# Zero-weight column-tiled matmuls in TensorE's idle gaps, and score matmuls over 32 rows

## The chip, the cores and the metric

The kernel runs on one core of one Trainium2 chip. The metric is the device time of one execution in microseconds (us). The comparison is between the kernel as it stands (called before) and the kernel with one change (called after), on the same inputs.

## The reference, cut to what matters

Attention with 32 query heads that share one key and one value head, and a GELU MLP, both fed by the same layer norm and added to the input:

```python
def _A_ref(x, wq, wk, wv, wo):              # x: 1 x 2048 x 512, H = 32 heads of Dh = 16
    q = (x @ wq).reshape(B, S, H, Dh).transpose(0, 2, 1, 3)
    k = x @ wk                              # one key head, one value head
    v = x @ wv
    scores = jnp.einsum("bhqd,bkd->bhqk", q, k) * (Dh ** -0.5)
    p = _softmax(scores, axis=-1)
    o = jnp.einsum("bhqk,bkd->bhqd", p, v)
    return o.transpose(0, 2, 1, 3).reshape(B, S, H * Dh) @ wo

def _B_ref(x, w1, b1, w2, b2):              # w1: 512 x 1792, w2: 1792 x 512
    h = _gelu(jnp.einsum("bsd,df->bsf", x, w1) + b1)
    return jnp.einsum("bsf,fd->bsd", h, w2) + b2

xn = _layernorm(x, axis=-1)
return x + _A_ref(xn, ...) + _B_ref(xn, ...)
```

Everything is bfloat16 outside. The exponentials of the scores are 32 x 2048 x 2048 elements, and they are the bulk of the elementwise work.

## The kernel before: how the work is tiled and ordered

**Stages.** A prologue (to about 45 us) normalises x, transposes it into `xnT`, and makes the keys `KT`, the values `V1` and the first queries `QT`. Then the main loop runs to about 857 us, and a short tail projects and stores the last tiles.

**The main loop.** Queries go in 4 blocks of 512 and heads in 8 groups of 4, so there are 32 groups (`gg`). One group has 64 score tiles: 16 key tiles of 128 by 4 heads. A tile is 128 keys x 512 queries and fills one PSUM bank. Three tiles make one unit `u`, and there are 683 units. `scores(u)` (line 660) is three matmuls of 17 rows, one for each of three heads, which lie in different 32-row strips of the array: rows `q0` to `q0 + 17` of `KT` and `QT`, where the 17th row carries a bound on the maximum and the rest of the 32 rows of `KT` and `QT` hold zeros. Even units write banks 0 to 2, odd units banks 3 to 5. `exp(u)` (line 680) is one ScalarE instruction over the two or three tiles of the unit that go to ScalarE (1024 or 1536 columns, written to `E`). At most one tile of a unit is marked `is_d` and goes to VectorE instead: `p1` (line 703) turns its scores into an integer whose bits are a rough exponential, and `close_batch` (line 717) adds four shifted copies, so that five matmuls make up a better one. Either way the tile is then multiplied by the values in `pv_mm` (line 712): a matmul that uses one of four 32-column strips of the array (a column-tiled matmul) and adds to bank 6, `pO`. Four such matmuls, one to each strip, run side by side.

**Side work.** The other column-tiled matmuls go through `mm4` (line 448) to bank 7, `pM`: the queries of later groups (`q_group`, `q_m`), the first MLP product (`h_mm`), the second with the output projection (`out_tile`, `y_tile`, `part_tile`). Each `pM` result is read out by a VectorE instruction with `allow=EV_ALLOW` (-2.0), a priority ahead of most other VectorE work but behind `p1` (`P1_ALLOW`, -20). At the end of a group `o_evac` (line 734) copies `pO` out on VectorE, and a chain of small DMAs on SyncE's queue brings the reciprocal of the denominators back for the normalisation. The GELU runs as a Tanh on ScalarE over up to 1536 columns (line 804), between the exponentials.

**What sets the order.** All engines run in order. The order is made when the program is built, by a planner of its own: `Prog.add` (line 59) records each operation with an assumed duration `occ`, latency `lat` and an `allow`; `Prog.schedule` (line 148) plays these forward in time, engine by engine, and `pick_pe` (line 117) chooses TensorE's next operation: scores first, column-tiled work in between, and no column-tiled work when a score is due within `S_WAIT`. A column-tiled matmul counts 0.216 us of its strip, a change between row-tiled scores and column-tiled work counts `SWITCH`. The planner of before takes TensorE as always at full clock. `Prog.emit` then writes the waits. There is a hook for filler matmuls (lines 190 to 201 and 959 to 961), which `FILL_GAP = 0` leaves off:

```python
        if FILL_GAP:
            pr.filler = lambda e: e.matmul(pO, zeros[:], xnT[:, 0, 0:TBW], start=False, stop=False, skip_group_check=True)
```

Of the kernel before, what the change touches and what calls it, by code (L numbers as in the profile page):

```python
# [10 lines left out]
P = 128  # L11
# [6 lines left out]
SPL_D = -107.78043958019079  # L18
SPL_MIN = 64.0
SWITCH = 0.1  # L20

ETA = 0.97
D_LEAD = 0.0
D_PEN = 0.3
D_TAIL = 10
D_FIRST = 3
FILL_GAP = 0
PV_MIN = 2
PV_S = 1
P1_ALLOW = -20.0  # L30
EV_ALLOW = -2.0
S_WAIT = 0.1
P_WAIT = 0.0
NE_ND_KB = (20,8,3)


class _Op:
    __slots__ = ("eng", "fn", "deps", "sdeps", "stream", "amt", "need", "ticket", "waits", "clock", "occ", "lat",
                 "allow", "kind", "tag", "nun", "outs", "rel", "rdy", "start", "end", "vis", "idx", "done")


class Prog:
# [5 lines left out]
    def __init__(self, nc):  # L48
        self.nc = nc
        self.ops = []  # L50
        self.writer = {}
        self.readers = {}
        self.accs = {}
        self.chain = {}
        self.in_chain = True
        self.filler = None
        self.fill_gap = None

    def add(self, eng, fn, r=(), w=(), acc=None, dma=None, occ=0.1, lat=0.15, allow=1.0, kind=None, tag=None, after=()):
# [88 lines left out]
    def schedule(self):  # L148
# [10 lines left out]
        ready = {e: [] for e in engs}  # L159
# [5 lines left out]
        mode = None  # L165
        cgbusy = [0.0] * 4
        visit = 0
        pend = 0.0
        accn = {}
        for op in ops:  # L170
# [7 lines left out]
        while left:  # L178
# [8 lines left out]
            e, t = best_e, best_t  # L187
            cand = [o for o in ready[e] if o.rdy <= t + 1e-9]
            if e == "pe":
                if self.filler is not None and opened is not None and t - free["pe"] > self.fill_gap and free["pe"] > 5:  # L190
                    f = _Op()
                    f.eng, f.stream, f.amt, f.need, f.ticket, f.deps, f.kind = "pe", "pe", 1, False, None, [], "fill"
                    f.fn = self.filler
                    f.start = max([free["pe"]] + cgbusy)
                    f.occ = 0.21
                    f.end = f.vis = f.start + f.occ
                    free["pe"] = f.end
                    mode = "full"
                    order.append(f)
                    nfill += 1  # L200
                    continue
                op = self.pick_pe(t, cand, ready["pe"], mode, visit, cgbusy)
# [12 lines left out]
            if e == "pe":  # L215
                st = t
                if op.kind in ("pv", "side"):
                    cg = op.tag[1]
                    st = max(t, cgbusy[cg], free["pe"])
                    if mode != "col":  # L220
                        st = max([t, pend + SWITCH] + [c + SWITCH for c in cgbusy])
                    op.start = st
                    cgbusy[cg] = st + 0.216
                    op.end = st + 0.006
                    op.vis = st + op.occ + op.lat
                    mode = "col"
                    g = op.tag[0]
                if op.kind == "pv":
                    n = accn[g] = accn[g] - 1
                    s = started.setdefault(g, {})  # L230
                    s[cg] = s.get(cg, 0) + 1
                    op.tag = (g, cg, s[cg] == 1)
                    if len(s) == 4:
                        opened = g
                    if n == 0:
                        opened = None
                elif op.kind != "side":
# [4 lines left out]
                    op.end = st + op.occ  # L242
                    op.vis = op.end + op.lat
                    if m == "col":
# [27 lines left out]
        self.nfill = nfill  # L272
        self.span = max(o.vis for o in order)
        self.ops = order

# [44 lines left out]
def bass_parallel_sum__grouped_kv_mqa__dense_activation_gelu__prompt_kernel(  # L320
# [34 lines left out]
    with ExitStack() as es:  # L355
# [276 lines left out]
                 r=["V1", "Vf"], w=[("V", 1 + v)])  # L632
        warm(4, 3)

        pool(lambda e: e.memset(zeros[:], 0.0), w=["zeros"])
# [24 lines left out]
        def scores(u):  # L660
            ts = list(range(3 * u, min(3 * u + 3, NTILE)))
            x = u % 2
            pieces, r = [], ["KTall"]
            for i, t in enumerate(ts):
                gg, kt, j = tile_of(t)
                tb, g = divmod(gg, NGR)
                q0 = 32 * j
                pieces.append((bank(3 * x + i), KT[q0:q0 + 17, kt * P:(kt + 1) * P], QT[q0:q0 + 17, g, :], q0))
                r += [("KT", kt // 4), ("QT", g), ("QTm", g, j)]

            def fn(e):
                for o, l, rh, q0 in pieces:
                    ins = e.matmul(o, l, rh, start=True, stop=True, tile_position=(q0, 0))  # L673
                return ins
            return add("pe", fn, r, [B(3 * x + i) for i in range(3)], occ=0.216, lat=0.22, allow=-1.0, kind="S")
# [281 lines left out]
            store(tb, i)  # L957
        pr.in_chain = False
        if FILL_GAP:
            pr.filler = lambda e: e.matmul(pO, zeros[:], xnT[:, 0, 0:TBW], start=False, stop=False, skip_group_check=True)  # L960
            pr.fill_gap = FILL_GAP
        fin = add("sp", None, r=[("ob", i) for i in range(4)], after=list(pr.ops))
        pr.schedule()
        global LAST
# [30 lines left out]
```

## Time and profile before

| what | value |
|---|---|
| time, median of 3 runs (873.56, 880.84, 873.33) | 873.56 us |
| the profiled execution's own time | 878.26 us |
| its span, first to last instruction | 876.4 us (1.9 us lie around it) |
| mean granted TensorE clock | 0.934 |
| busy: PE, VectorE (DVE), ScalarE (ACT) | 801.6, 751.7, 788.6 us |
| chain that ended last, by engine | ACT 51%, PE 33%, DVE 14% |

How to read it: PE's busy time is modelled with each matmul's pipeline latency, so a full share does not mean full use. The granted clock (PEclk) is the share of full speed that TensorE's clock gate let through in a stretch; it reads 1.00 or 0.50, or a mean over both. In the chain of work that ended last, the exponentials (L692) have 49% of the span. "Idle before" is the time that an engine stood still ahead of an instruction, with the engine whose result ended it.

### The profile page before, as it was taken

Reading aid. Unit: us, or ns where it says so; the run is one execution under the profiler, and the core shown is the slowest. Engines: PE = TensorE matmul, PEld = TensorE weight load, DVE = VectorE, ACT = ScalarE, POOL = GpSimd, SP = SyncE. Lnnn points to the kernel's source line nnn. Section 1 sums busy time; section 2 is a strip of 40 time slices with the busy share of each in tenths; the row PEclk is TensorE's granted clock in tenths of the full one; section 3 lists DMA queues with packets and bytes.
Section 4 is the critical chain, followed back from the end, with each engine's and each line's share of the span. In section 5 each row is a group of like instructions: output and inputs, shape, how many; then the busy total and the mean of one; then the engine's idle time right before and its main releaser. Section 6 shows DMA issues by size and latency. Waiting matters only on the chain.

```text
span 876.4 us, 20514 instructions
## 1 busy us (share of the span) xinstructions
PE 801.6 (91%) x8766; PEld 238.4 (27%) x8768; DVE 751.7 (86%) x1429; ACT 788.6 (90%) x731; POOL 25.5 (3%) x51
## 2 busy tenths in 40 slices
PE   3788999999899999998989999989989999999997
PEld 1312222222222322322222322322222332222223
DVE  7259897887988869999998968999889968999985
ACT  3378999889999899999999999999899999999981
POOL 7030000000000000000000000000000000000000
PEclk9668998779889999999999999998889999999999
DMA  8000000000000010000000100000000000000000
GB/s 289 1 25 3 15 13 14 13 15 14 2 14 20 21 26 9 21 2 14 15 13 15 27 20 9 15 14 14 15 14 15 26 20 8 15 15 14 15 14 25
DMA packets 23971, 19.02 MB, mean 22 GB/s; under 512 B 12369, under 2 KB 19402, under 8 KB 23882
## 3 DMA queue, kind: packets, MB, share of 16 engines
q1 hardware_dynamic: 22826, 17.69, 7.0%
q8 instruction: 69, 1.13, 0.5%
q10 hardware_dynamic: 1056, 0.03, 0.1%
q14 instruction: 20, 0.16, 0.1%
HBM read 14.98 MB, written 2.35 MB: 20 GB/s over the span
## 4 chain that ended last, share of the span: by engine, by line
ACT 51%; PE 33%; DVE 14%; issue 1%; DMA 0%; DVEq 0%; ACTq 0%
ACT E L692 49%; PE pAll L713 12%; PE pAll L451 10%; PE pAll L673 9%; DVE Dt L709 4%; DVE Dt L723 4%; PE pAll L445 2%; ACT ub L804 1%; DVE hb L790 1%; ACT xnT L544 1%; DVE stats L503 1%; DVE Of L736 0%; DVE ub L806 0%; DVE ub L801 0%; DVE ub L803 0%
## 5 line engine op out<-in xcount | busy, mean ns | idle before, releaser
L692 ACT ACTIVATE E<-pAll 128x1024 bf16<-128x1024 f32 (+1 forms) x683 | 751.2, 1295 | 44.7 <-PE pAll L673 39.9
L713 PE MATMUL pAll<-Dt,V 128*32 128x512 bf16 x2075 | 340.4, 401 | 2.5 <-DVE Dt L709 1.2
L709 DVE TENSOR_SCALAR Dt<-pAll 128x512 int16<-128x512 f32 x415 | 278.6, 682 | 60.7 <-PE pAll L673 56.6
L673 PE MATMUL pAll<-QT,KT 17*128 17x512 bf16 x2048 | 277.5, 400 | 43.5 <-ACT E L692 36.7
L713 PE MATMUL pAll<-E,V 128*32 128x512 bf16 x1633 | 309.1, 404 | 2.0 <-DVE Of L736 1.4
L723 DVE TENSOR_SCALAR Dt<-Dt 128x1536 int16<-128x1536 int16 (+2 forms) x588 | 282.8, 525 | 1.0
L673 PEld LDWEIGHTS pAll<-QT,KT 17*128 17x128 bf16 x2048 | 67.5, 91 | 329.2 <-ACT E L692 276.0
L713 PEld LDWEIGHTS pAll<-Dt,V 128*32 128x32 bf16 x2075 | 93.5, 98 | 98.4 <-issue 46.8
L451 PE MATMUL pAll<-w_sb,ub 128*32 128x512 bf16 x896 | 111.0, 391 | 0.0
L713 PEld LDWEIGHTS pAll<-E,V 128*32 128x32 bf16 x1633 | 74.3, 96 | 76.6 <-issue 56.4
L451 PE MATMUL pAll<-xnT,w_sb 128*32 128x512 bf16 x896 | 81.2, 400 | 1.3 <-DVE hb L790 1.0
L451 PE MATMUL pAll<-wop,oT 128*32 128x512 bf16 x512 | 70.1, 381 | 1.9 <-DVE x_sb L839 1.9
L451 PE MATMUL pAll<-xnT,wqp 128*32 128x512 bf16 x496 | 50.1, 442 | 0.5 <-DVE hb L790 0.3
L790 DVE TENSOR_SCALAR hb<-pAll,b1T 128x512 bf16<-128x512 f32 x56 | 41.3, 737 | 7.3 <-PE pAll L451 7.2
L451 PEld LDWEIGHTS pAll<-w_sb,ub 128*32 128x32 bf16 x896 | 28.8, 96 | 25.6 <-issue 15.9
L575 DVE CAST QT<-pAll 128x512 bf16<-128x512 f32 x32 | 21.8, 683 | 13.9 <-PE pAll L451 10.1
L804 ACT ACTIVATE ub<-ub 128x1536 bf16<-128x1536 bf16 (+1 forms) x20 | 30.6, 1531 | 0.0
L451 PEld LDWEIGHTS pAll<-xnT,w_sb 128*32 128x32 bf16 x896 | 21.2, 97 | 30.8 <-issue 15.1
L451 PEld LDWEIGHTS pAll<-wop,oT 128*32 128x32 bf16 x512 | 20.0, 95 | 15.7 <-issue 5.9
L541 PE MATMUL pAll<-ident,ub 128*128 128x128 bf16 x64 | 8.2, 282 | 14.9 <-POOL ub L527 10.7
L736 DVE COPY Of<-pAll 128x512 f32<-128x512 f32 x31 | 21.1, 680 | 0.1
L747 DVE TENSOR_TENSOR oT<-Of,rbc 128x512 bf16<-128x512 f32 x31 | 21.0, 679 | 0.0
(91 smaller groups left out, 254.1 us busy)
## 6 DMA issues: line engine op xcount, KB each, us to landing
rbc<-rden_rows SPq DMA_DIRECT2D x124, 64.0 KB, 2.0
w_sb<-in_B_w_dram SPq DMA_DIRECT2D x2, 1792.0 KB, 12.1
x_sb<-in_A_x_dram SPq DMA_DIRECT2D x8, 256.0 KB, 4.7
out_dram<-x_sb SPq DMA_DIRECT2D x16, 128.0 KB, 1.7
QT<-mT SPq DMA_DIRECT2D x60, 2.0 KB
ub<-in_A_wq_dram SPq DMA_DIRECT2D x1, 512.0 KB, 6.5
wop<-in_A_wo_dram SPq DMA_DIRECT2D x4, 128.0 KB, 2.7
den<-Of SPq DMA_DIRECT2D x31, 8.0 KB
```

The costliest lines, as they stand in the source:

```text
L445: return add("pe", lambda e: e.matmul(o, l, rh, start=start, stop=stop, **kw), r, w, occ=occ, lat=0.23, allow=allow, kind=kind, tag=tag)
L451: add("pe", lambda e, c=c, j=j: e.matmul(o[c, :], l[:, c], rh, start=start, stop=stop, tile_position=(0, 32 * j)), r, [(k, j) for k in w] ...
L575: dve(lambda e: e.tensor_copy(QT[:, hq, :], bank(bk)), w=[B(bk)] + [(B(bk), j) for j in range(4)] + [ ("QT", hq)] + [("QTm", hq, j) for j ...
L673: ins = e.matmul(o, l, rh, start=True, stop=True, tile_position=(q0, 0))
L692: exps.append(act(lambda e: e.activation(E[:, s0:s0 + na, :], bank(b0, na).rearrange("p (a n) -> p a n", a=na), ACT.Exp, scale=LN2 / 128.0 ...
L709: dve(lambda e: e.tensor_scalar(Dt[:, KZ, s, :], bank(bk), float(127 * 128) + SPL_D, SPL_MIN, ALU.add, ALU.max), w=[B(bk), ("D", s, KZ)], ...
L713: add("pe", lambda e, a, b: e.matmul(pO[32 * j:32 * j + 32, :], V1[:, v, kt, :], rhs, start=a, stop=b, tile_position=(0, 32 * j)), r=r + [ ...
L723: dve(lambda e, k=k: e.tensor_scalar(Dt[:, k, s0:s0 + n, :], Dt[:, KZ, s0:s0 + n, :], float(SPL_K[k]), None, ALU.add), r=[("D", s0 + i, KZ ...
L736: dve(lambda e: e.tensor_copy(Of[:, i, :], pO), w=["O", ("Of", i)], allow=0.0)
L747: onorm[gg] = dve(lambda e: e.tensor_tensor(oT[:, gg % NOT, :], Of[:, i, :], rbc[:, i, :], ALU.mult), r=[("Of", i)] + [("rbc", i, j) for j ...
L790: dve(lambda e: e.tensor_scalar(hb[:, ft % 6, :], pM, b1T[:, ft:ft + 1], None, ALU.add), r=["b1T"], w=M4 + [("h", ft % 6)], allow=EV_ALLOW)
L804: act(lambda e: e.activation(uu, uu, ACT.Tanh, scale=GELU_K), r=uk, w=uk, n=c, allow=2.5, kind="tanh")
```

## The change

The fillers are switched on and made over, the score matmuls take all 32 rows of their strip, and the planner follows a model of the clock gate. The words that come with the change also say that `pM` is read out first on VectorE.

- **Fillers.** A filler is now a set of four matmuls, one to each 32-column strip, with 128 x 32 zeros as weights and 512 columns of `xnT` as data. Where a group has `pO` open in all four strips it adds zero to `pO`; otherwise, where the last operation on `pM` was a VectorE read that has finished, it writes zeros to `pM`. The planner puts a set wherever, in its own time, TensorE would otherwise wait more than `FILL_GAP` = 0.25 us for the next score, less than `FILL_U` = 0.8 of the last `WIN` = 3.413 us was used (a column-tiled matmul counts a quarter of its 0.2133 us, a unit's scores 0.75 of theirs), and the time is past `FILL_FROM` = 60.
- **The clock in the planner.** The planner counts the same use in fixed windows of 3.413 us and doubles TensorE's durations in the window behind one with less than `HAM_T` = 0.35. So the order of the other work moves a little as well.
- **Scores.** `KT[q0:q0+32]` and `QT[q0:q0+32]` in place of 17 rows. The added rows are zero in both.

The program has 576 fillers, 144 sets. No other instruction is added or removed on any engine.

```diff
+WIN = 3.413
+HAM_T = 0.35
+HAM_PHASE = 1.5
-FILL_GAP = 0
+FILL_GAP = 0.25
+FILL_U = 0.8
+FILL_FROM = 60.0
...
+        op.pm = any(k == ("bank", 7) or k[0] == ("bank", 7) for k in w)
...
             if e == "pe":
-                if self.filler is not None and opened is not None and t - free["pe"] > self.fill_gap and free["pe"] > 5:
-                    f = _Op()
...
+                op = self.pick_pe(t, cand, ready["pe"], mode, visit, cgbusy)
+                st = max([free["pe"]] + cgbusy) if mode == "col" else max([free["pe"], pend + SWITCH] + cgbusy)
+                while recent and recent[0][0] < st - WIN:
+                    recent.pop(0)
+                low = sum(a for _, a in recent) < FILL_U * WIN
+                lim = min([o.rdy for o in ready["pe"] if o.kind == "S"] + [t + 9.0]) if op is None else t
+                tgt = pO_open = opened is not None
+                if not tgt and pmev is not None and pmev.vis <= st:
+                    tgt = True
+                if FILL_GAP and op is not None and isinstance(op, float):
+                    tgt = False
+                if FILL_GAP and tgt and low and st > FILL_FROM and lim - st > FILL_GAP:
+                    for cg in range(4):
+                        f = _Op()
...
+                        f.deps = list(self.fill_deps) if pO_open else self.fill_deps + [pmev]
+                        f.fn = (lambda e, cg=cg, o=pO_open: self.filler(e, cg, o))
+                        f.occ = 0.216 * slow
...
             if e == "pe":
-                pend = op.start + op.occ
+                while op.start > wend:
+                    slow = 1.0 if area > HAM_T * WIN else 2.0
+                    ncold += slow > 1
+                    area, wend = 0.0, wend + WIN
+                pend = op.start + op.occ * slow
...
+            if op.pm:
+                pmev = op if e == "dve" else None
+                if pmev is not None:
+                    op.need = True
...
-                pieces.append((bank(3 * x + i), KT[q0:q0 + 17, kt * P:(kt + 1) * P], QT[q0:q0 + 17, g, :], q0))
+                pieces.append((bank(3 * x + i), KT[q0:q0 + 32, kt * P:(kt + 1) * P], QT[q0:q0 + 32, g, :], q0))
...
         if FILL_GAP:
-            pr.filler = lambda e: e.matmul(pO, zeros[:], xnT[:, 0, 0:TBW], start=False, stop=False, skip_group_check=True)
+            pr.filler = lambda e, j, o: e.matmul((pO if o else pM)[32 * j:32 * j + 32, :], zeros[:, 0:32], xnT[:, 0, 0:TBW],
+                                                 start=not o, stop=not o, skip_group_check=True,
+                                                 tile_position=(0, 32 * j))
```

Two places on TensorE show what this does to the order. In the rows, `QT,KT` are scores (three matmuls are one unit), `E,V` and `Dt,V` are `pv_mm`, `xnT,w_sb` is the first MLP product, `w_sb,ub` the second, and `xnT,zeros` are the fillers.

The first place is the 87th unit, around 151 us of the profile, where a Tanh on ScalarE holds the next scores up. TensorE before:

```order
L673 MATMUL pAll<-QT,KT 128x512 x3
L713 MATMUL pAll<-Dt,V 32x512 x3
L713 MATMUL pAll<-E,V 32x512
L713 MATMUL pAll<-Dt,V 32x512 x5
L713 MATMUL pAll<-E,V 32x512
L673 MATMUL pAll<-QT,KT 128x512 x3
L713 MATMUL pAll<-E,V 32x512 x4
L673 MATMUL pAll<-QT,KT 128x512 x3
```

TensorE after, from the second of those scores:

```order
L717 MATMUL pAll<-QT,KT 128x512 x3
L757 MATMUL pAll<-E,V 32x512 x4
L1004 MATMUL pAll<-xnT,zeros 32x512 x32
L717 MATMUL pAll<-QT,KT 128x512 x3
L757 MATMUL pAll<-E,V 32x512 x3
L1004 MATMUL pAll<-xnT,zeros 32x512 x4
L717 MATMUL pAll<-QT,KT 128x512 x3
L1004 MATMUL pAll<-xnT,zeros 32x512 x4
```

Eight filler sets stand between the four value matmuls and the next scores, and one set more behind each of the two units that follow.

The second place is the 344th unit, around 456 us, at the end of a group. TensorE before, where four units of scores stand next to each other:

```order
L673 MATMUL pAll<-QT,KT 128x512 x3
L713 MATMUL pAll<-E,V 32x512 x3
L673 MATMUL pAll<-QT,KT 128x512 x12
L713 MATMUL pAll<-E,V 32x512
L673 MATMUL pAll<-QT,KT 128x512 x3
L451 MATMUL pAll<-w_sb,ub 32x512 x12
```

TensorE after:

```order
L717 MATMUL pAll<-QT,KT 128x512 x3
L757 MATMUL pAll<-E,V 32x512 x3
L1004 MATMUL pAll<-xnT,zeros 32x512 x4
L717 MATMUL pAll<-QT,KT 128x512 x3
L1004 MATMUL pAll<-xnT,zeros 32x512 x4
L757 MATMUL pAll<-E,V 32x512
L717 MATMUL pAll<-QT,KT 128x512 x3
L1004 MATMUL pAll<-xnT,zeros 32x512 x8
L757 MATMUL pAll<-E,V 32x512 x3
L757 MATMUL pAll<-Dt,V 32x512
```

Here sets have come in, and value matmuls stand between scores that followed each other directly before.

More of the change, by code (lines that the diff above doesn't have):

```diff
@@ L33 @@
 P_WAIT = 0.0
-NE_ND_KB = (20,8,3)
+NE_ND_KB = (20, 8, 3)
 class _Op:
     __slots__ = ("eng", "fn", "deps", "sdeps", "stream", "amt", "need", "ticket", "waits", "clock", "occ", "lat",
-                 "allow", "kind", "tag", "nun", "outs", "rel", "rdy", "start", "end", "vis", "idx", "done")
+                 "allow", "kind", "tag", "nun", "outs", "rel", "pm", "rdy", "start", "end", "vis", "idx", "done")
 class Prog:
@@ L57, in __init__ @@
         self.fill_gap = None
+        self.fill_deps = []
+        self.log = []
     def add(self, eng, fn, r=(), w=(), acc=None, dma=None, occ=0.1, lat=0.15, allow=1.0, kind=None, tag=None, after=()):
@@ L167, in schedule @@
         visit = 0
+        recent = []
+        pmev = None
+        area, wend, slow = 0.0, HAM_PHASE, 2.0
+        ncold = 0
         pend = 0.0
@@ L189, in schedule @@
             if e == "pe":
-                if self.filler is not None and opened is not None and t - free["pe"] > self.fill_gap and free["pe"] > 5:
-                    f = _Op()
[L192 to L199, printed above, removed]
+                op = self.pick_pe(t, cand, ready["pe"], mode, visit, cgbusy)
@@ new lines, in schedule @@
+                if FILL_GAP and op is not None and isinstance(op, float):
[3 more added lines that the diff above has]
+                        f = _Op()
+                        f.eng, f.stream, f.amt, f.need, f.ticket, f.kind = "pe", "pe", 1, False, None, "fill"
+                        f.deps = list(self.fill_deps) if pO_open else self.fill_deps + [pmev]
+                        f.fn = (lambda e, cg=cg, o=pO_open: self.filler(e, cg, o))
+                        f.tag = (None, cg)
+                        f.occ = 0.216 * slow
+                        f.start, f.end, f.vis = st, st + 0.006, st + f.occ
+                        order.append(f)
+                        recent.append((st, 0.0533))
+                        cgbusy[cg] = st + f.occ
+                    area += 0.2133
+                    pend = st + f.occ
+                    mode = "col"
+                    free["pe"] = max(free["pe"], st + 0.02)
@@ L200, in schedule @@
                     nfill += 1
                     continue
-                op = self.pick_pe(t, cand, ready["pe"], mode, visit, cgbusy)
+                if op == "idle":
+                    op = None
                 if op is None or isinstance(op, float):
@@ L222, in schedule @@
                     op.start = st
-                    cgbusy[cg] = st + 0.216
+                    cgbusy[cg] = st + 0.216 * slow
+                    area += 0.0533
+                    recent.append((st, 0.0533))
                     op.end = st + 0.006
-                    op.vis = st + op.occ + op.lat
+                    op.vis = st + op.occ * slow + op.lat
                     mode = "col"
@@ L241, in schedule @@
                     op.start = st
-                    op.end = st + op.occ
+                    op.end = st + op.occ * slow
                     op.vis = op.end + op.lat
+                    area += op.occ * (0.75 if op.kind == "S" else 1.0)
+                    recent.append((st, op.occ * (0.75 if op.kind == "S" else 1.0)))
                     if m == "col":
@@ L272, in schedule @@
         self.nfill = nfill
+        self.ncold = ncold
         self.span = max(o.vis for o in order)
@@ L633, in bass_parallel_sum__grouped_kv_mqa__dense_activation_gelu__prompt_kernel @@
         warm(4, 3)
-        pool(lambda e: e.memset(zeros[:], 0.0), w=["zeros"])
+        zop = pool(lambda e: e.memset(zeros[:], 0.0), w=["zeros"])
         pool(lambda e: e.memset(wop[:], 0.0), w=["wop"])
```

3 lines of the change are left out of this document (added).

## The prediction

> **What bounds the kernel now.** I read the page first, then the groups of instructions by line with shapes kept apart, then busy time in stretches cut where the granted clock changes. The page's head, its ScalarE row, and the two exponential groups (behind the bar: busy us, mean ns, then idle us before them and what ended it):
>
> ```profile
> span 876.4 us, 20514 instructions
> PE 801.6 (91%) x8766; PEld 238.4 (27%) x8768; DVE 751.7 (86%) x1429; ACT 788.6 (90%) x731; POOL 25.5 (3%) x51
> ACT  3378999889999899999999999999899999999981
> PEclk9668998779889999999999999998889999999999
> L692 ACT ACTIVATE E<-pAll 128x1024 bf16<-128x1024 f32 x416 | 416.0, 1133 | 20.5 <-PE pAll L673 19.9 <-PE pAll L713 0.4
> L692 ACT ACTIVATE E<-pAll 128x1536 bf16<-128x1536 f32 x267 | 388.7, 1549 | 24.2 <-PE pAll L673 20.0 <-PE pAll L713 3.6
> ```
>
> ScalarE sets the pace: it does exponentials almost without a break, and what breaks it is TensorE's scores (L673), 19.9 + 20.0 us. So only those breaks can be won, about 45 us in all. The clock row says where to look: TensorE's clock is below full in the first half and again before three quarters.
>
> In a finer cut the granted clock is 0.50 or 1.00 for whole stretches of 3.413 us on one fixed grid. Four of those stretches in a row, by busy time (columns: stretch, its length, PE, PEld, DVE, ACT, POOL busy, clock, DMA share, GB/s):
>
> ```profile
> 232.70:236.11 3.41, 1.42 (x12) 0.32 (x9) 3.41 (x7) 3.41 (x5) 0.00 (x0) 1.00 0.00 0
> 236.11:239.52 3.41, 3.04 (x23) 0.81 (x27) 3.26 (x7) 3.41 (x4) 0.00 (x0) 0.50 0.02 5
> 239.52:242.94 3.42, 3.42 (x33) 1.01 (x29) 2.85 (x6) 1.69 (x3) 0.00 (x0) 0.50 0.04 4
> 242.94:246.35 3.41, 3.41 (x43) 0.85 (x35) 2.38 (x4) 3.41 (x4) 0.00 (x0) 1.00 0.24 77
> ```
>
> In the first TensorE idles more than half of the time, while ScalarE never does (3.41 of 3.41): there is simply nothing for TensorE to do. The next two stretches run at half clock. Then work has piled up and ScalarE starves: 1.69 of 3.42. So idle time of an engine that does not bound is paid for one or two stretches later.
>
> Behind 62 us there are 14 such entries. The busiest and the least busy, the sum row of all 14, and the two least busy stretches that were not followed by half clock:
>
> ```profile
> 181.50:184.91 3.41, 2.36 (x23) 0.65 (x23) 3.38 (x7) 3.41 (x5) 0.00 (x0) 1.00 0.02 2
> 457.98:461.39 3.41, 1.22 (x10) 0.38 (x10) 3.41 (x7) 3.41 (x5) 0.00 (x0) 1.00 0.00 0
> sum 47.78, PE 27.06 PEld 7.33 DVE 46.15 ACT 47.29 POOL 0.00; mean PE 1.93 PEld 0.52 DVE 3.30 ACT 3.38 POOL 0.00
> 533.07:536.48 3.41, 2.48 (x29) 0.64 (x26) 3.40 (x7) 3.41 (x5) 0.00 (x0) 1.00 0.02 5
> 809.55:812.96 3.41, 2.51 (x22) 0.69 (x22) 3.41 (x8) 3.41 (x4) 0.00 (x0) 1.00 0.02 2
> ```
>
> No entry has over 2.36 us of PE, no other stretch under 2.48. That is the threshold I use: 2.4 us busy out of 3.41. [...]
>
> **What half clock costs.** I cut 75.68 to 857.34 us into the 14 half-clock stretches, each with one full-clock stretch behind it, and the 15 stretches between. The sum row of each:
>
> ```profile
> sum 133.13, PE 129.42 PEld 33.90 DVE 107.67 ACT 109.01 POOL 0.00; mean PE 9.24 PEld 2.42 DVE 7.69 ACT 7.79 POOL 0.00
> sum 648.53, PE 605.02 PEld 179.63 DVE 592.55 ACT 634.66 POOL 0.00; mean PE 40.33 PEld 11.98 DVE 39.50 ACT 42.31 POOL 0.00
> ```
>
> ScalarE idles 133.13 - 109.01 = 24.1 us in the first and 648.53 - 634.66 = 13.9 us (2.1%) in the second. At 2.1% the first would idle 2.8 us. So half clock costs up to 21.3 us.
>
> **The change, part by part. Fillers.** 144 sets, all beside ScalarE's exponentials. What a set takes, and what room it has, from the timeline (start us, us, engine, instruction, idle before):
>
> ```profile
> 151.51 0.61 PE L713 MATMUL pAll<-E,V 128*32 128x512 bf16 x4
> 152.33 2.42 ACT L692 ACTIVATE E<-pAll 128x1536 bf16<-128x1536 f32 x2
> 153.89 0.39 PE L673 MATMUL pAll<-QT,KT 17*128 17x512 bf16 x3 [1.78 <-ACT E L692]
> ...
> 210.28 0.59 PE L713 MATMUL pAll<-E,V 128*32 128x512 bf16 x2
> 210.50 0.59 PE L713 MATMUL pAll<-Dt,V 128*32 128x512 bf16 x2
> ...
> 257.07 0.39 PE L673 MATMUL pAll<-QT,KT 17*128 17x512 bf16 x3 [0.20 <-ACT E L692]
> 257.39 0.40 PE L713 MATMUL pAll<-E,V 128*32 128x512 bf16 x3
> 257.99 0.39 PE L673 MATMUL pAll<-QT,KT 17*128 17x512 bf16 x3 [0.20 <-ACT E L692]
> ```
>
> Rounds of column-tiled matmuls follow each other at 0.22 us (210.28, 210.50), and scores to column-tiled work takes 0.32 us (257.07, 257.39). So a set costs 0.22 us in a run and up to 0.32 with a switch: 144 x 0.22 = 32 us to 144 x 0.32 = 46 us of TensorE, if none were hidden. The place with most room: behind the matmuls at 151.51 the next scores start at 153.89, 2.38 us later; the changed order puts eight sets there, 8 x 0.22 = 1.76 us, and with the round's own 0.22 and the way back to scores, 0.32, that is 2.30 us, inside it. In the ordinary unit (257.07 to 257.99, 0.92 us) scores, one round and the way back take 0.64; a set makes that 0.86. It fits with 0.06 us to spare. And a late score is not at once a late exponential, since the other three banks hold one exponential's work (at least 0.92 us, the spacing of these scores) and scores take 0.39. So I cost hidden sets at nothing; if the planner misplaces a fifth of them by 0.3 us beyond this cover, 29 x 0.3 = 9 us comes back. I take 1 us. They add no wait that matters: only the first of all waits for GpSimd's zeros, which are long there, and one for a VectorE read.
>
> Do they lift the stretches over 2.4 us? Counting the changed order's sets in the units that each of the 14 entries holds gives 2, 3, 5, 9, 2, 6, 4, 0, 1, 5, 7, 5, 4, 1, in order of time. At 0.22 us each, the ten with two or more sets behind 100 us go from 1.42 to 2.36 us to 2.74 or more. Four are short or on the line: 75.68 (1.36 + 0.44), 410.19 (1.96, no set), 457.98 (1.22 + 0.22), 836.86 (2.27 + 0.22). In the first three other matmuls move in as well, as in the second place shown with the change. Three of these entries, and the half-clock stretches behind the four:
>
> ```profile
> 75.68:79.10 3.42, 1.36 (x13) 0.45 (x13) 3.38 (x6) 3.42 (x5) 0.00 (x0) 1.00 0.01 2
> 410.19:413.60 3.41, 1.96 (x24) 0.48 (x21) 3.41 (x7) 3.41 (x4) 0.00 (x0) 1.00 0.00 0
> 836.86:840.27 3.41, 2.27 (x16) 0.72 (x16) 3.33 (x7) 3.41 (x5) 0.00 (x0) 1.00 0.00 0
> ...
> 79.10:89.34 10.24, 9.65 (x101) 2.65 (x99) 9.04 (x19) 7.85 (x8) 0.00 (x0) 0.67 0.04 9
> 413.60:420.43 6.83, 6.83 (x80) 2.18 (x77) 5.42 (x11) 5.66 (x6) 0.00 (x0) 0.75 0.04 5
> 461.39:468.22 6.83, 6.83 (x79) 1.92 (x80) 5.70 (x12) 5.30 (x6) 0.00 (x0) 0.75 0.02 4
> 840.27:847.10 6.83, 6.83 (x84) 2.06 (x85) 6.12 (x13) 3.84 (x4) 0.00 (x0) 0.75 0.02 4
> ```
>
> They idle 2.39 + 1.17 + 1.53 + 2.99 = 8.1 us, 7.4 above the 2.1%. The other ten hold 21.3 - 7.4 = 13.9 us. Taking half of the four: 13.9 + 3.7 = 17.6 us.
>
> Not all of that returns. Where column-tiled work bunches up (here 62 matmuls in one stretch), ScalarE starves at full clock too:
>
> ```profile
> 488.70:492.11 3.41, 3.41 (x62) 1.37 (x54) 2.76 (x7) 1.34 (x2) 0.00 (x0) 1.00 0.12 16
> ```
>
> 2.07 us lost in one full-clock stretch. Several of the 14 hold such a burst. I take off a quarter, 4.4 us, and 1.2 us of half clock that starts in new places, since the order and the grid both shift. 17.6 - 4.4 - 1.2 - 1 = 11 us.
>
> **Scores over 32 rows.** Three matmuls of 17 rows take 400 ns each, column-tiled ones over 128 rows 401:
>
> ```profile
> L673 PE MATMUL pAll<-QT,KT 17*128 17x512 bf16 x2048 | 277.5, 400 | 43.5 <-ACT E L692 36.7
> L713 PE MATMUL pAll<-Dt,V 128*32 128x512 bf16 x2075 | 340.4, 401 | 2.5 <-DVE Dt L709 1.2
> ```
>
> So rows cost no time: 0. They might count as more activity for the gate, which no row shows; bounds 0 and the four doubtful entries' other half, 3.7 us. I take 0.
>
> **`pM` read out first.** The diff holds nothing for it: `EV_ALLOW` is -2.0 in both. 0. **The order of the rest** shifts by a few matmuls and comes back together every ten to twenty units: 0, bounds 2 us each way. **The first 62 us** get no set and keep their half clock.
>
> **Sum.** 878.3 (the profiled execution's own time) - 11 = 867. But that execution is 4.7 us above the median of 873.56. If the 4.7 us is half clock that the other runs had less of, the changed kernel still comes to 867; if it is something else, to 862.6. [...] I take a point between, nearer the lower: **864 us**, 1.1% faster.
>
> **Rivals.** (1) *The sets do not count.* The gate may weigh what switches in the array, and zero weights give products of zero. Speaks for it: nothing in the trace has zero weights. Against it: no row hints at data. Then the 14 entries stay and only the order moves: 871 to 876, point 873.6. [...] (2) *Slower: sets stand ahead of due scores.* Place: the low-use units, where 44 of the 98 runs of sets in the changed order stand directly behind scores. If ScalarE's real pace leaves less room than the planner's, each such set delays scores by 0.32 us, and that decides from the point where the delay passes the cover of 0.92 - 0.39 = 0.53 us, so from two sets too many in one unit. A third of the sets late and no gain: 48 x 0.32 = 15 us, 889. With the gain it cancels. Against it: at 151.51 and 257.07 the room fits the planner's count. (3) *All half clock goes*, the 32 rows helping, and the bursts dissolve with it: 878.3 - 21.3 = 857, less 4 us if the first 62 us profit: 853.
>
> **How the numbers follow.** Forecast 0.56 (its own range 858 to 870), rival (1) 0.22, rival (2) 0.10, rival (3) 0.12. The range 853 to 876 leaves out rival (2) and the tails. One per cent is about what a measurement of this kernel can tell from no change. Faster by over 1% (under 864.8): two thirds of the forecast, 0.38, and 0.12 of rival (3), with a little of (1): 0.51. Slower by over 1%: most of rival (2), 0.09. Within: 0.40.
>
> **What would show it.** Right: mean clock at 0.97 or more, few half-clock stretches between 62 and 857 us, ScalarE's idle time before L692 down from 44.7 to about 33 us, PE matmuls up by 576. Wrong: as many half-clock stretches as before in spite of the sets (rival 1); ScalarE waiting for scores in stretches at full clock right behind sets (rival 2).

## The result, and the profile after

The changed kernel takes 847.65 us (median of 4 runs, 844.26 to 848.22) beside 873.44 us before (873.22 to 880.84). The ratio is 0.9677, with a 95% interval of 0.962 to 0.9733: 3.2% faster. The forecast was 864 us with a range of 853 to 876. So the direction was right, and the gain, 26 us, was more than twice the 9.6 us forecast and lies outside the range. Of the kernel with the order alone, further down, three of four runs lie more than 1.5% above its fastest; such slow runs, its profiled one of 904.01 us among them, carry no conclusion here.

The changed kernel's page, by the lines that were shown of before (its profiled execution took 847.98 us):

```profile
span 846.2 us, 21678 instructions
PE 801.3 (95%) x9344; PEld 244.0 (29%) x9344; DVE 748.3 (88%) x1429; ACT 784.2 (93%) x731; POOL 25.5 (3%) x51
PEclk9899999999999999999999999999999999999999
ACT 63%; PE 29%; DVE 5%; POOL 1%; issue 1%; DMA 0%; ACTq 0%; DVEq 0%
```

The clock row has no low slice left behind the prologue; the mean granted clock went from 0.934 to 0.992. In the chain that ended last, ScalarE's share rose from 51% to 63%. The groups, with shapes kept apart (behind the bar: busy us, mean ns | idle before, and what ended it):

```profile
L736 ACT ACTIVATE E<-pAll 128x1024 bf16<-128x1024 f32 x416 | 419.4, 1176 | 3.1 <-PE pAll L717 3.1
L736 ACT ACTIVATE E<-pAll 128x1536 bf16<-128x1536 f32 x267 | 392.0, 1578 | 16.4 <-PE pAll L717 12.2 <-PE pAll L757 4.2
L717 PE MATMUL pAll<-QT,KT 32*128 32x512 bf16 x2048 | 267.9, 386 | 18.6 <-ACT E L736 13.8 <-DVE Dt L753 0.8 <-DVE hb L834 0.5
L1004 PE MATMUL pAll<-xnT,zeros 128*32 128x512 bf16 x576 | 62.2, 383 | 0.0
```

Idle time before the exponentials fell from 44.7 to 19.5 us. The 576 fillers keep TensorE busy for 62.2 us, which it did not have before: its total is 801.3 against 801.6, because the real matmuls run faster (scores 386 ns each in the mean, against 400).

The stretch from the first exponential's start to the last one's end carries nearly the whole difference, 29.5 of the spans' 30.2 us; the tail behind it is 17.7 us in both. Before, by busy time in stretches (stretch, length, PE, PEld, DVE, ACT, POOL, clock, DMA share, GB/s):

```profile
44.72:858.69 813.97, 764.08 (x8428) 221.26 (x8428) 719.88 (x1349) 771.99 (x703) 8.55 (x9) 0.94 0.06 15
```

After:

```profile
44.04:828.50 784.46, 762.87 (x9004) 226.33 (x9004) 716.45 (x1349) 767.57 (x703) 8.55 (x9) 1.00 0.06 16
```

This part is 29.5 us shorter: ScalarE's idle time went from 42.0 to 16.9 us (25.1 us), and its busy time from 771.99 to 767.57 (4.4 us) for the same 703 instructions. On the grid of 3.413 us there were 29 half-clock stretches in this part before, and there are 2 after, at 47 and 569 us. The second, with the stretches around it:

```profile
562.43:565.84 3.41, 2.42 (x30) 0.76 (x30) 3.41 (x8) 3.41 (x4) 0.00 (x0) 1.00 0.02 2
565.84:569.26 3.42, 2.00 (x25) 0.56 (x26) 3.42 (x7) 3.42 (x4) 0.00 (x0) 1.00 0.00 0
569.26:572.67 3.41, 3.41 (x29) 0.61 (x30) 3.17 (x7) 2.65 (x4) 0.00 (x0) 0.50 0.32 78
572.67:576.08 3.41, 3.41 (x52) 0.92 (x44) 3.06 (x7) 3.39 (x4) 0.00 (x0) 1.00 0.03 7
```

With 2.00 us of PE the clock falls; with 2.42 it does not. The forecast's threshold of 2.4 us held here. And the clock returns after a single stretch, although that one had hardly more matmuls in it (29) than stretches of before that were followed by more half clock (23 to 27 in the first three of the four shown further down).

### The profile page after: what moved, and what is told of

It reads as the page before. It is cut to its first block, busy times and chain, and to the rows that moved or that the text cites. A ratio compares the mean times of both kernels' runs of the same rounds, so it can differ in the third digit from the quotient of the medians.

```text
span 846.2 us, 21678 instructions
## 1 busy us (share of the span) xinstructions
PE 801.3 (95%) x9344; PEld 244.0 (29%) x9344; DVE 748.3 (88%) x1429; ACT 784.2 (93%) x731; POOL 25.5 (3%) x51
## 4 chain that ended last, share of the span: by engine, by line
ACT 63%; PE 29%; DVE 5%; POOL 1%; issue 1%; DMA 0%; ACTq 0%; DVEq 0%
ACT E L736 60%; PE pAll L757 9%; PE pAll L495 8%; PE pAll L717 8%; ACT ub L848 2%; PE pAll L489 2%; DVE Dt L753 2%; DVE Dt L767 2%; PE pAll L1004 1%; ACT xnT L588 1%; DMA wk_s<-in_A_wk_dram 0%; POOL ub L571 0%; DVE x_sb L883 0%; PE pAll L585 0%; ACT KT L598 0%
## 5 line engine op out<-in xcount | busy, mean ns | idle before, releaser
L736 ACT ACTIVATE E<-pAll 128x1024 bf16<-128x1024 f32 (+1 forms) x683 | 747.4, 1333 | 19.5 <-PE pAll L717 15.3
L757 PE MATMUL pAll<-Dt,V 128*32 128x512 bf16 x2075 | 334.4, 384 | 1.0 <-DVE Dt L767 0.2
L757 PE MATMUL pAll<-E,V 128*32 128x512 bf16 x1633 | 297.5, 385 | 1.4 <-DVE Of L780 1.0
L717 PE MATMUL pAll<-QT,KT 32*128 32x512 bf16 x2048 | 267.9, 386 | 18.6 <-ACT E L736 13.8
L717 PEld LDWEIGHTS pAll<-QT,KT 32*128 32x128 bf16 x2048 | 67.4, 91 | 299.3 <-ACT E L736 267.3
L757 PEld LDWEIGHTS pAll<-Dt,V 128*32 128x32 bf16 x2075 | 91.1, 95 | 94.9 <-issue 41.4
L495 PE MATMUL pAll<-w_sb,ub 128*32 128x512 bf16 x896 | 109.2, 383 | 0.0
L495 PE MATMUL pAll<-xnT,w_sb 128*32 128x512 bf16 x896 | 78.9, 385 | 0.6 <-DVE hb L834 0.3
L1004 PE MATMUL pAll<-xnT,zeros 128*32 128x512 bf16 x576 | 62.2, 383 | 0.0
L495 PE MATMUL pAll<-xnT,wqp 128*32 128x512 bf16 x496 | 46.3, 389 | 0.1
```

The costliest lines, as they stand in the source:

```text
L495: add("pe", lambda e, c=c, j=j: e.matmul(o[c, :], l[:, c], rh, start=start, stop=stop, tile_position=(0, 32 * j)), r, [(k, j) for k in w] ...
L736: exps.append(act(lambda e: e.activation(E[:, s0:s0 + na, :], bank(b0, na).rearrange("p (a n) -> p a n", a=na), ACT.Exp, scale=LN2 / 128.0 ...
L757: add("pe", lambda e, a, b: e.matmul(pO[32 * j:32 * j + 32, :], V1[:, v, kt, :], rhs, start=a, stop=b, tile_position=(0, 32 * j)), r=r + [ ...
L1004: pr.filler = lambda e, j, o: e.matmul((pO if o else pM)[32 * j:32 * j + 32, :], zeros[:, 0:32], xnT[:, 0, 0:TBW], start=not o, stop=not o ...
```

## The experiments

Three things changed at once: filler sets, scores over 32 rows, and the planner's order. The first theory gives the gain to the sets. The second gives it to the rows, the third to the order. The first four kernels take them apart. Each group of four ran on one chip beside the kernel before, whose median was 878.04, 878.33 and 874.64 us in the three groups, so the ratios are what to compare.

### Rows alone

```diff
 before.py
-                pieces.append((bank(3 * x + i), KT[q0:q0 + 17, kt * P:(kt + 1) * P], QT[q0:q0 + 17, g, :], q0))
+                pieces.append((bank(3 * x + i), KT[q0:q0 + 32, kt * P:(kt + 1) * P], QT[q0:q0 + 32, g, :], q0))
```

> The kernel before with scores over 32 rows in place of 17, nothing else. Theory 1 (the filler sets hold TensorE's clock, each half-clock stretch of 3.41 us costs about 1.0 us): 871 to 876 us, clock 0.93 to 0.94. Theory 2 (the 32 rows count as more activity for the clock gate and carry the gain): under 858 us, clock 0.97 or more. Theory 3 (the changed order of the other work carries it): 873 us.

Measured: 860.85 us (855.53 to 863.58), ratio 0.9792 (0.9711 to 0.9873), clock 0.960 in the profile. Fifteen zero rows in each score matmul take 2.1% off the time, which neither the forecast nor the first theory had. The second theory's 858 us is not reached either. How the rows act can be seen where the two kernels still do the same work, near 48 us. Before, a half-clock stretch and the one behind it:

```profile
48.38:51.79 3.41, 3.41 (x27) 0.53 (x19) 1.02 (x2) 3.41 (x4) 3.33 (x4) 0.50 0.02 5
51.79:55.20 3.41, 3.16 (x19) 0.58 (x19) 1.66 (x4) 2.43 (x3) 2.19 (x3) 0.50 0.11 37
```

With 32 rows:

```profile
48.10:51.52 3.42, 3.42 (x27) 0.57 (x19) 0.99 (x2) 3.42 (x4) 3.34 (x4) 0.50 0.03 5
51.52:54.93 3.41, 3.13 (x35) 0.89 (x32) 2.00 (x4) 2.92 (x3) 2.20 (x3) 1.00 0.12 34
```

Both first stretches hold 27 matmuls, six of them scores, and read as busy throughout. With 17 rows half clock goes on for three more stretches; with 32 rows it ends.

### Everything but the rows

```diff
 after.py
-                pieces.append((bank(3 * x + i), KT[q0:q0 + 32, kt * P:(kt + 1) * P], QT[q0:q0 + 32, g, :], q0))
+                pieces.append((bank(3 * x + i), KT[q0:q0 + 17, kt * P:(kt + 1) * P], QT[q0:q0 + 17, g, :], q0))
```

> The changed kernel with scores over 17 rows again. Theory 1: 848 to 852 us, clock 0.98 or more. Theory 2: 862 to 873 us, clock 0.95 or less. Theory 3: 848 us.

Measured: 862.51 us (857.47 to 862.59), ratio 0.9813 (0.9749 to 0.9878), clock 0.963. Sets with 17-row scores (and with the changed order) give about as much as 32 rows without sets. The trace shows again what the rows do. In this kernel the clock falls five times in the main loop, but one of the falls lasts seven stretches. The fall and the seven, with the stretch that ends them:

```profile
565.45:568.86 3.41, 2.27 (x23) 0.56 (x21) 3.41 (x6) 3.41 (x5) 0.00 (x0) 1.00 0.01 3
568.86:572.28 3.42, 3.42 (x30) 0.72 (x26) 3.42 (x8) 3.42 (x4) 0.00 (x0) 0.50 0.02 2
572.28:575.69 3.41, 3.41 (x29) 0.71 (x29) 3.41 (x8) 3.35 (x4) 0.00 (x0) 0.50 0.03 2
575.69:579.10 3.41, 3.41 (x30) 0.49 (x22) 2.77 (x6) 2.43 (x3) 0.00 (x0) 0.50 0.26 82
579.10:582.52 3.42, 3.42 (x34) 0.65 (x26) 2.60 (x6) 2.44 (x3) 0.00 (x0) 0.50 0.00 0
582.52:585.93 3.41, 3.41 (x34) 0.77 (x30) 1.33 (x3) 2.43 (x3) 0.00 (x0) 0.50 0.00 0
585.93:589.34 3.41, 3.41 (x34) 0.60 (x30) 2.08 (x4) 2.06 (x2) 0.00 (x0) 0.50 0.00 0
589.34:592.76 3.42, 3.42 (x33) 0.74 (x30) 2.27 (x5) 2.02 (x2) 0.00 (x0) 0.50 0.02 7
592.76:596.17 3.41, 3.41 (x35) 0.99 (x32) 3.41 (x9) 3.19 (x4) 0.00 (x0) 1.00 0.00 0
```

TensorE reads as busy for the whole of each of the seven, and the clock stays at half. ScalarE works only 2.0 to 2.4 of 3.41 us in five of them. The same place in a kernel with 32-row scores is the stretch at 569.26 us shown of the changed kernel: busy throughout as well, 29 matmuls, and the clock returns. A second example, from the kernel with rows alone:

```profile
222.18:225.60 3.42, 1.60 (x13) 0.54 (x13) 3.42 (x8) 3.42 (x5) 0.00 (x0) 1.00 0.02 5
225.60:229.01 3.41, 3.41 (x35) 1.12 (x34) 3.24 (x7) 3.41 (x3) 0.00 (x0) 0.50 0.02 2
229.01:232.42 3.41, 3.41 (x49) 0.95 (x41) 2.82 (x6) 2.51 (x4) 0.00 (x0) 1.00 0.10 29
```

35 matmuls at half clock, and it is back; with 17 rows a stretch of 34 was not enough. Counted over the main loops of the profiles, by half-clock stretches that were at least 95% busy and held two or more units of scores: with 17 rows 16 of 22 were followed by another (7 of 10 before, 9 of 12 in this kernel). With 32 rows it was 1 of 24 (0 of 7 in the rows alone, 1 of 17 in the changed kernel, its repetition, the order with rows, the half and the double sets, the early matmuls). Later kernels give 1 of 5 with 32 rows (no clock model, `FILL_U` 0.5), 3 of 6 with 24 rows, and 2 of 7 where the sets use only 32 rows.

### Order and rows without sets, and with half of the sets

```diff
 after.py, order and rows without sets
-                        f.fn = (lambda e, cg=cg, o=pO_open: self.filler(e, cg, o))
+                        f.fn = None
```

> The changed kernel with its order and its 32 rows, but no filler matmul is issued; all real work stands in the order that the planner made with them. Theory 1: 868 to 878 us, clock about 0.93. Theory 2: 848 to 855 us, clock 0.98. Theory 3: 848 to 855 us at a clock of about 0.93.

Measured: 856.59 us (854.67 to 857.66), ratio 0.9758 (0.9698 to 0.9818), clock 0.968. No theory's numbers are met. The second comes nearest, with a range that ends 1.6 us lower and a clock of 0.98. The first, which had no gain here, is furthest off: most of the gain stands without a single filler. Against rows alone (0.9792) the order adds little, and the two intervals overlap.

```diff
 after.py, half of the sets
-                        f.fn = (lambda e, cg=cg, o=pO_open: self.filler(e, cg, o))
+                        f.fn = (lambda e, cg=cg, o=pO_open: self.filler(e, cg, o)) if nfill % 2 == 0 else None
```

> The changed kernel with every second filler set left out, 72 sets in place of 144. Theory 1: between, 855 to 863 us, clock 0.95 to 0.98, and the time falls with the number of half-clock stretches at about 1 us each. Theories 2 and 3: 848 us, as the changed kernel.

Measured: 850.08 us (846.76 to 852.69), ratio 0.9684 (0.962 to 0.9747), clock 0.978. Half of the sets do what all do, within what can be told. So the first theory falls, but for its price of about 1 us a half-clock stretch: sets and rows work on the same thing, and the rows alone, or the sets with the changed order, each give more than half.

That thing is the number of half-clock stretches, and theory A puts the whole time down to it. The next four kernels test that, against theory B, in which sets and order have prices of their own.

### The changed kernel again, and double sets

> The changed kernel once more, beside the three others on one chip, so that differences of a few us can be read. Theory A (time is 844 us plus 1.1 us for each half-clock stretch of 3.41 us between the first and the last exponential; sets and order cost nothing by themselves): 844 to 850 us with 0 to 5 such stretches. Theory B (144 sets cost about 5 us by themselves, the planner's order gives about 4 us): the same.

Measured: 849.11 us (848.43 to 850.48), ratio 0.9675 (0.9624 to 0.9726), 4 half-clock stretches between the first and the last exponential.

```diff
-                        f.fn = (lambda e, cg=cg, o=pO_open: self.filler(e, cg, o))
+                        f.fn = (lambda e, cg=cg, o=pO_open: (self.filler(e, cg, o), self.filler(e, cg, o))[1])
```

> Every filler set issued twice (288 sets in the places of 144), so that each overruns the room that the planner gave it by 0.22 us. Theory A: the extra is covered by the exponential that is still running, 844 to 850 us, within 2 us of the changed kernel. Theory B: about 5 us more than the changed kernel, 850 to 856 us. If scores are held up by their full length (144 x 0.22 us): 875 us or more.

Measured: 865.98 us (865.34 to 867.92), ratio 0.9869 (0.9817 to 0.9922), with the clock at 0.986. Neither theory's number: 17 us over the changed kernel, of 144 x 0.22 = 32 us that the second sets take. Where it went, in the double sets' groups:

```profile
L736 ACT ACTIVATE E<-pAll 128x1024 bf16<-128x1024 f32 x416 | 412.9, 1101 | 9.8 <-PE pAll L717 8.5
L736 ACT ACTIVATE E<-pAll 128x1536 bf16<-128x1536 f32 x267 | 382.7, 1524 | 21.6 <-PE pAll L717 16.6 <-PE pAll L757 4.5
```

and in its main loop:

```profile
43.59:845.64 802.05, 783.92 (x9580) 243.34 (x9580) 719.54 (x1349) 773.19 (x703) 8.54 (x9) 0.99 0.06 15
```

ScalarE waits for scores again, 31.4 us before the exponentials against 19.5 in the changed kernel's first profile, and is busy for 773.19 us against 767.57, at a clock of 0.99 against 1.00. So about half of the overrun is covered, and half is paid. The room that the planner found was real, and there is little beyond it.

### The order alone, and early matmuls

The order alone is the changed kernel with both edits from above: no filler issued, and 17 rows.

> The planner's changed order alone: no filler issued, scores over 17 rows. Theory A: order does nothing by itself, but the gate may drop at other places; 868 to 878 us at a clock of 0.93 to 0.95, and on the line of 844 + 1.1 us per half-clock stretch. Theory B: 4 us under the kernel before at the same clock.

Measured: 871.34, 896.03, 900.82 and 904.01 us, at clocks of 0.939, 0.918, 0.909 and 0.902. Only the first can be compared. Before, in the same group, took 872.98 to 881.80 us at clocks of 0.951 to 0.932. One run is too few: what the order does by itself with 17 rows is not settled, and theory B's 4 us is neither shown nor refuted.

```diff
         warm(4, 3)
+        warm(6, 7)
 
         zop = pool(lambda e: e.memset(zeros[:], 0.0), w=["zeros"])
```

> The changed kernel with six further matmuls (identity weights, into the bank that nothing uses yet) behind the first six scores, where TensorE waits for the first exponentials. Theory A: the half-clock stretches between 44 and 62 us go (1 in the profile of the changed kernel, more in others), 843 to 848 us, 0 to 3 us under the changed kernel. If the six hold the third scores up instead: 1 to 2 us over it.

Measured: 848.95 us (848.93 to 849.36), ratio 0.9673 (0.9613 to 0.9733): no change against 849.11, and 1 us over theory A's range. The half-clock stretch near 50 us is gone in its profile, but there are two others, at 367 and 565 us, as many as in the changed kernel's first profile.

### What the gate counts, and which parts are needed

```diff
 before.py
-                pieces.append((bank(3 * x + i), KT[q0:q0 + 17, kt * P:(kt + 1) * P], QT[q0:q0 + 17, g, :], q0))
+                pieces.append((bank(3 * x + i), KT[q0:q0 + 24, kt * P:(kt + 1) * P], QT[q0:q0 + 24, g, :], q0))
```

> The kernel before with scores over 24 rows, 7 zero rows more than before and 8 fewer than the 32. Theory R (the gate counts a score matmul by its rows, zeros included): about half of what the 32 rows gave, 864 to 872 us, clock 0.945 to 0.955. Theory S (it counts the whole 32-row strip only when all of its rows are named): no change, 873 to 878 us.

Measured: 866.35 us (863.92 to 868.71), ratio 0.9864 (0.9778 to 0.995): between before and 32 rows, as theory R says. The interval overlaps that of the 32 rows alone (0.9711 to 0.9873), but not 1, so theory S falls.

```diff
 after.py
-HAM_T = 0.35
+HAM_T = -1.0
```

> The changed kernel with a planner that takes TensorE as always at full clock (155 sets, 32 rows): the third part of the change undone. If the planner's clock model gives nothing by itself: 846 to 851 us, as the changed kernel. If it is needed: 853 us or more.

Measured: 848.73 us (845.81 to 852.66), ratio 0.9671 (0.9598 to 0.9744). The planner's clock model gives nothing by itself. The order still moves with the sets here, so this is no test of the order as a whole.

```diff
 after.py
-FILL_U = 0.8
+FILL_U = 0.5
```

> The changed kernel with sets only where the planner counts less than half of the last 3.413 us as used (78 sets in place of 144). If sets in well-used places are spare: 846 to 850 us, and at most 2 us under the changed kernel, since the sets cost at most that by themselves. If they are needed: 851 us or more at a clock under 0.98.

Measured: 849.15 us (846.9 to 852.0), ratio 0.9675 (0.9604 to 0.9745). 78 sets in the less used places do what 144 do.

```diff
 after.py
-            pr.filler = lambda e, j, o: e.matmul((pO if o else pM)[32 * j:32 * j + 32, :], zeros[:, 0:32], xnT[:, 0, 0:TBW],
+            pr.filler = lambda e, j, o: e.matmul((pO if o else pM)[32 * j:32 * j + 32, :], zeros[0:32, 0:32], xnT[0:32, 0, 0:TBW],
```

> The changed kernel with filler sets over 32 rows in place of 128: 32 x 32 zeros as weights, 32 rows of data, the same time on TensorE. Theory R (activity goes by rows): a set counts a quarter, and the time goes most of the way to that without sets, 853 to 858 us. If any matmul counts alike, whatever its rows: 847 to 850 us.

Measured: 854.78 us (852.0 to 862.75), ratio 0.9731 (0.9651 to 0.9812), close to that without sets (0.9758). By time alone this is not clear, since the interval reaches down to the changed kernel's 0.9675, and the profiled run, with 862.75 us, was the longest of five. The trace decides. The sets are as many and as long (391 ns a matmul against 383), and they do little for the clock: 0.962 in the profile, beside 0.968 in that of the order and rows without sets and 0.992 in the changed kernel's. A stretch of it, and the one behind:

```profile
621.86:625.27 3.41, 3.41 (x42) 1.10 (x43) 3.41 (x8) 2.70 (x3) 0.00 (x0) 1.00 0.00 0
625.27:628.69 3.42, 3.42 (x31) 0.73 (x27) 2.22 (x5) 2.90 (x2) 0.00 (x0) 0.50 0.04 7
```

and the fillers' part of the first, by the busy time of line L1004 alone (PE, PEld):

```profile
621.86:625.27 3.41, 1.93 (x28) 0.62 (x32) 1.00 0.00 0
```

TensorE reads as busy for all of 3.41 us at full clock with 42 matmuls, 28 of them 32-row fillers (1.93 us), and the clock falls. In the changed kernel it did not fall behind 2.42 us and 30 matmuls (562.43 us, above). Before, the busiest stretch that fell behind 62 us had 2.36 us, in the changed kernel 2.00.

### One line through all of them

Half-clock stretches between the first exponential's start and the last one's end, and the length of that part, from each profile:

| kernel | half-clock stretches | main loop, us |
|---|---|---|
| no clock model | 1 | 785.1 |
| changed | 2 | 784.5 |
| early matmuls | 2 | 784.7 |
| changed, again | 4 | 786.4 |
| `FILL_U` 0.5 | 5 | 786.3 |
| half of the sets | 6 | 787.7 |
| order and rows, no sets | 10 | 790.6 |
| sets over 32 rows | 14 | 798.6 |
| rows alone | 15 | 798.7 |
| sets and order, 17 rows | 16 | 798.8 |
| 24 rows | 23 | 807.0 |
| before | 29 | 814.0 |
| order alone, 17 rows | 50 | 840.3 |
| double sets | 3 | 802.1 |

A straight line through the first twelve is 782.1 us + 1.08 us per half-clock stretch, and none lies more than 2.3 us off it. The order alone is not used for the line; it lies 4 us above it. The double sets lie 17 us above it. So theory A holds for these twelve, at its price of 1.1 us, as long as the sets fit their gaps. That sets and order cost nothing by themselves holds within these 2.3 us: the order and rows without sets lie 2.3 us below the line, the sets over 32 rows 1.3 us above it.

## Why the prediction was right or wrong

- **The bound and the place.** Right. ScalarE sets the pace, the gain came from its waits for scores, and it came with the half clock. The clock fell behind stretches of low use: 1.22 to 2.36 us of PE out of 3.41 before (behind 62 us), 2.00 in the changed kernel, 1.60 in the rows alone (at 222 us).
- **The threshold of 2.4 us of PE out of 3.41.** It held for before and for the changed kernel (2.00 us fell, 2.42 stayed), but it is a stand-in, and it moves with the rows: in the rows alone 2.21 and 2.33 us stayed at full clock (at 99 and 372 us) and the highest that fell had 2.12; with sets and 17 rows 2.65 us fell (at 719 us). Busy time alone does not decide the fall: 3.41 us busy at full clock fell when the fillers had 32 rows (at 621 us).
- **"They might count as more activity for the gate, which no row shows ... I take 0".** This step failed. Rows alone took 17 us off (860.85 against 878.04), over four times the upper bound of 3.7. On top of the sets they are worth about 12 us (0.9677 against 0.9813 without them, in different groups), most of the 16 us by which the forecast was off. The bound was drawn from the falls alone, in the four doubtful entries. The rows change both the falls (the highest that fell had 2.12 us in the rows alone, 2.36 before) and the return (counted as above, another half-clock stretch followed in 1 of 24 cases with 32 rows, in 16 of 22 with 17). That busy time does not decide the return could be read in the trace of before. Four half-clock stretches in a row there, by busy time:

```profile
184.91:188.32 3.41, 3.41 (x23) 0.72 (x21) 2.64 (x7) 3.41 (x4) 0.00 (x0) 0.50 0.01 2
188.32:191.74 3.42, 3.42 (x27) 0.72 (x24) 3.35 (x6) 2.96 (x4) 0.00 (x0) 0.50 0.31 55
191.74:195.15 3.41, 3.41 (x27) 0.52 (x26) 1.86 (x4) 2.46 (x2) 0.00 (x0) 0.50 0.09 29
195.15:198.56 3.41, 3.41 (x22) 0.74 (x19) 2.32 (x4) 2.01 (x3) 0.00 (x0) 0.50 0.00 0
```

  TensorE reads as busy throughout, and the clock is at half for all four, which no threshold on busy time explains: full clock follows the fourth, which has the fewest matmuls. I did not ask why.
- **What half clock costs.** Mis-sized. The forecast had 21.3 us for 25 stretches behind 62 us, 0.85 each. The line gives 1.08 each, and 27 stretches fewer make 29 us, against 29.5 us measured in the main loop. Two parts were missed. ScalarE's busy time fell by 4.4 us too. One exponential does not read shorter (1176 ns against 1133 of the smaller kind), but more of them overlap the instruction ahead: 56 of the 703 instructions started with ScalarE standing still before, 17 after, so a start from standstill costs more than the idle time in front of it, by an estimate from these two profiles 4.4 / 39 = 0.11 us. And the first 62 us, taken as 0: the 21st exponential starts at 72.7 us before and at 67.4 after, with four half-clock stretches from 48 us before and one after. The rows alone do this as well (68.4), as the pair of stretches at 48 us shows.
- **"I take off a quarter, 4.4 us"** for bursts that starve ScalarE at full clock too, half of the four doubtful entries (3.7 us), and 1.2 us for new places. The first two were wrong in one direction: ScalarE idles 16.9 of 784.46 us after, 2.2%, the share that full-clock stretches had before, and the half clock behind all four doubtful entries is gone. The third was about right: one half-clock stretch, at 569 us, is in a new place.
- **Sets cost nothing where they fit.** Right, with 1 us taken: the changed kernel and its repetition lie within 0.3 us of the line. The reason given was half right. The cover of 0.53 us behind a late score was overstated. In the trace of the changed kernel the sets stand in 95 units, 63 of them with one set and 22 with two; at 0.22 us more for each set, only the ten units with three or more overrun 0.53 us, by some 3 us in all, and the double sets cost 17.
- **Order, 0.** Not refuted, and not settled. The planner's clock model is worth nothing (848.73 us without it against 849.11 with it, in different groups, ratios 0.9671 and 0.9675). The order with rows and without sets is 4.3 us under the rows alone, with overlapping intervals, and with 17 rows there is one run to go by. **`pM` read out first, 0.** Nothing in the diff, and nothing was tried.
- **Run to run.** In runs of before on the chips of the experiments, 871.85 us came with a clock of 0.947 and 882.89 with 0.930. The spread goes with half clock, which the forecast had left open.
- **Rivals.** That the sets do not count fell: with 17-row scores and all zero weights, sets bring the time to 862.51, under the best run of the same order without them (871.34). Sets that hold scores up were seen only where they are doubled. The third rival, all half clock gone with the rows helping, is what happened. It had a chance of 0.12 and 853 us, and it too gave less gain than was measured, because of the price.

What stays open is the gate's exact measure. Rows count, with zeros in them (24 rows give a ratio of 0.9864, 32 rows 0.9792; fillers over 32 rows give 0.9731, over 128 rows 0.9677 and none 0.9758); whether columns count in the same way, and how concurrent strips add up, was not tried.

No kernel here beats the changed one beyond the measurement. The line without any half clock gives 782.1 us for the main loop against 784.5, so the clock has 2 us left to give, no more than the line's own spread.

## What to carry to other kernels

Where a slower engine feeds on TensorE, count the half-clock stretches and price them from traces with different counts, before discounting anything: here each cost about 1.1 us of 3.41. Matmuls that use few rows can keep TensorE busy throughout and still leave the clock at half (with 17-row scores 3.41 of 3.41 us at 0.50, seven stretches in a row), so padding them with zero rows, where that costs no time (400 ns with 17 rows, 393 with 32), comes first, and fillers over all rows go only into gaps that the trace shows. Ask of a throttled state not only what starts it but what it takes to leave it.

## What the runs showed of the hardware

- Busy time, as the profile models it, does not decide the clock alone: two stretches with 27 matmuls each (at 48 us), of which only the one with 32-row scores was followed by full clock; seven half-clock stretches in a row with 3.41 of 3.41 us busy (17-row scores), and a fall right after 3.41 us busy (fillers over 32 rows). The rows that a matmul uses weigh in: of the half-clock stretches that were at least 95% busy and held two or more units of scores, 16 of 22 were followed by another with 17 rows, 1 of 24 with 32.
- Zeros count. Rows of zeros in both operands brought the clock back, and weights of zeros held it: the clock was 0.960 with 32-row scores against 0.934 with 17, and 0.992 with sets added to the 32 rows against 0.968 with the same order and none.
- 17, 24 and 32 rows took the same time per score matmul but for the clock: 400, 397 and 393 ns at mean clocks of 0.934, 0.951 and 0.960, and with 17 rows and sets 394 ns at 0.963.
